# Other steps for the transform pieces of batches one to four and other banks for all of them, in a fused Fourier filter and PReLU feed-forward kernel

## Chip, cores and metric

One core of a Trainium2 chip runs the whole program in one launch. The metric is device time of that launch in microseconds (us). Engines are named PE (matrix multiply; PEld is its weight load), DVE (vector), ACT (scalar), POOL (GpSimd) and SP (sync, which here only issues DMAs). ACT, DVE and POOL run their own queues in order; SP and POOL issue the DMAs of their queues in order too.

## What is computed

```
X = rfft(x, axis=1)                      # x: 8 batches x 3008 positions x 256
y = irfft(X * (filt_r + 1j * filt_i), n=3008, axis=1)
h = y.reshape(24064, 256) @ w_in         # 256 -> 2048
g = maximum(h, 0) + alpha * minimum(h, 0)
out = g @ w_out                          # 2048 -> 256
```

Inputs and outputs are fp32; inside, operands are fp16 and sums fp32.

## The kernel before

**Feed-forward.** 24064 tokens are worked in 48 blocks of 512 tokens (every twelfth, the sixth of each pair of batches, has 384). A block takes 16 steps; step 16n+j computes the j-th group of 128 hidden units of block n (`Block.up`, L478: two 512-wide matmuls into `hps`, two steps share one PSUM tile of the pool psH, which has two). After each odd step ACT copies the pair to `gtb` as fp16 (L486), and DVE applies the PReLU (L489 twice, L490). The second product, by `wout_s`, is a list of single matmuls (`eight`, L515; in the 19 blocks named in FAST `seven`, L537, a variant with 7 products in place of 8, which needs sums from DVE, L498 and L500, and two accumulate DMAs on POOL for each half, L502 and L504). It runs 16 steps (LAG) behind: with each step one sixteenth of a block's list is issued. So block 0 has no such work beside it. Output tiles `osb` (ring of three) are stored by SP (L447).

**Fourier part.** Length 3008 is split as 47 x 64. A batch passes through pieces, each small enough to be put between two steps of the feed-forward:
- `load_x` (L148): POOL issues two DMAs for one of four chunks `xs`; the ring has four, so a chunk of the next batch waits for the same chunk of the batch before.
- `piece_a` (16 of them): one 512-wide matmul (L190) to a psF bank, evicted by ACT to `asb` (L260). After each fourth, `save_a` (SP) writes the chunk to `a_dram`; `asb` has two buffers. `turn_a` (SP) reads all back with positions on partitions, as `at`, in one part or in quarters.
- `piece_b` (12): two 256-wide matmuls (L210), then DVE multiplies the bank twice by the filter (`ww` L213, `uu` L214), and POOL adds `ww` with halves exchanged onto `uu` by two accumulate DMAs (L216). `uu` has four buffers. `ww` uses `filts_s` and `uu` uses `filt_s`, whose upper half must hold the negated lower one: `neg` (DVE, L626) in four parts makes this for batches from 1 on.
- `piece_c` (12): two matmuls by `twi_s` (L228) to a bank, evicted by ACT to `v`. After each third, `turn_c` (SP, four DMAs) writes `v_dram`; after the last of a batch, three loads of `zt` follow (`load_z`, ring of three), the fourth later.
- `piece_d` (16): four 94-wide matmuls (L253) to a bank, evicted by ACT to `yT` (128 features x tokens), which the feed-forward reads. Four of these serve 752 tokens.

Batch 0 has its own path (`First`), run ahead of the steps up to its first quarter of `yT`; of its remaining pieces, `piece_t` (transposes, L331) and `piece_d` 4 to 15, some are evicted by DVE in place of ACT. `combine` (DVE, five instructions) prepares sums of `wout_s` for the FAST blocks, whose first is block 12, at step 192.

**Order.** Everything is issued in program order by hand (`manual_schedule`). `plan` maps a step to a list of pieces; `put` appends to it. At a step, first come delayed stores, then the sums of FAST blocks, then the pieces of that step in the order in which they were put, then `up`, then the second product's share. Batches 4 to 7 repeat the lists STEPS_A, STEPS_B, STEPS_C, STEPS_D, shifted by 96 steps each; batches 1 and 2 go through `plan_fft` with regular spacings; batch 3 uses the lists with changed A and B. A batch b is needed from step 96b on.

**Banks.** The pieces of the transform share two PSUM banks, pools psF0 and psF1 with one buffer each. The string BANKS holds one digit for each piece in program order: which of the two it takes. A piece waits until the earlier one on its bank is evicted.

Of the kernel before, what the change touches and what calls it, by code (L numbers as in the profile page):

```python
# [16 lines left out]
NK1 = 24  # L17
D = 256
NB = 8
DFF = 2048  # L20
NH = 32
BANKS = (
    "010101010101010101010101010101001011011011011011011011011010101011010101010101010101010010101010"
    "101010101010101010101101101101010101001011010010110101010101101010101010101001101010101010101010"
    "101001010110101010101010101010101010100110100101010010110111010110101010101010101010101010101001"
    "010101010100101101101010010101010101010101010101010101100101101010110100100010100101010101010101"
    "01010101010101101010101101001110101010101010101010101010"
)
STEPS_A = (-84, -81, -77, -76, -65, -59, -58, -58, -56, -53, -52, -51, -50, -48, -46, -43)
STEPS_B = (-21, -15, 4, 6, 13, 21, 25, 27, 32, 40, 54, 55)  # L30
STEPS_C = (2, 10, 16, 19, 24, 33, 35, 46, 62, 63, 70, 70)
STEPS_D = (89, 89, 90, 91, 92, 94, 95, 98, 100, 101, 105, 113, 118, 125, 144, 147)
FAST = frozenset([n for n in range(12,42) if n%6 in (0,2,4)]+[42,43,44,45])
SUMS = ((9, 1, 0), (10, 3, 0), (16, 2, 0), (17, 1, 1), (17, 3, 1), (19, 2, 1), (20, 4, 0), (21, 4, 1))
TAIL = ((12, 1, 0), (12, 3, 0), (18, 1, 1), (18, 3, 1), (18, 2, 0), (18, 2, 1), (20, 4, 0), (21, 4, 1))
LAG = 16
# [44 lines left out]
def kernel(  # L81
# [10 lines left out]
    nc = tc.nc  # L92
# [48 lines left out]
    def xrow(b, h, c):  # L141
        return bass.AP(tensor=x.tensor, offset=x.offset + (b * NFFT + NH * h + 8 * c) * D,
                       ap=[[N2 * D, N1], [1, 8 * D]])

    def load_x(b, c):
        xs = p_x.tile([2 * N1, 8 * D], FP16, name="xs")
        for h in range(2):
            nc.gpsimd.dma_start(out=xs[h * N1 : h * N1 + N1], in_=xrow(b, h, c))  # L148
        return xs
# [115 lines left out]
    both = (on_act, on_dve)  # L265
# [71 lines left out]
    xc = {(0, c): load_x(0, c) for c in range(4)}  # L337
    f0 = First()
# [116 lines left out]
    def flush():  # L455
        for fn, args in late:
            fn(*args)
        late.clear()

    class Block:  # L460
        def __init__(self, n, p, t0, tn):
            self.n, self.p, self.t0, self.tn = n, p, t0, tn
            self.fast = n in FAST
            self.sent = 0
# [130 lines left out]
    def put(step, fn, *args):  # L595
        plan.setdefault(step, []).append((fn, args))

    def plan_fft(b, a0, ga, ta, b0, gap, add, lag, d0, quarters, x_at):
        f = Fft(b)
        for i in range(16):  # L600
            put(int(a0 + ga * i) - (b == 2 and i == 7), f.piece_a, i, on_act)
        for c in range(4):
            put(int(a0 + ga * (4 * c + 3)) - (b == 2 and c == 1), f.save_a, c)
            if b + 1 < NB:
                put(x_at[c],
                    lambda b=b, c=c: xc.update({(b + 1, c): load_x(b + 1, c)}))
        for q in range(quarters):
            w = NK1 // quarters
            put(ta, f.turn_a, nc.sync, w * q, w * q + w)
        bs = [b0 + (2 * int(gap * kp / 2) if add else int(gap * kp)) for kp in range(12)]  # L610
        for kp in range(12):
            put(bs[kp], f.piece_b, kp)
            put(bs[kp] + lag, f.piece_c, kp, on_act)
        for q in range(4):
            put(bs[3 * q + 2] + lag + 1, f.turn_c, q)
        for i in range(16):
            put(d0 + min(i, 4) + 2 * max(i - 4, 0), f.piece_d, i, on_act)
        put(d0 + 5, f.load_z, 3)

    for g, t0, d0, gap, evs in ((1, 0, 6, 1, both), (2, 17, 25, 2, (on_dve,)), (3, 32, 40, 2, (on_act,))):  # L620
        for i in range(4):
            put(t0 + gap * i, f0.piece_t, 4 * g + i, evs[i % len(evs)])
            put(d0 + gap * i, f0.piece_d, 4 * g + i, evs[i % len(evs)])

    def neg(ka, kb):
        nc.vector.tensor_scalar(filt_s[64:128, ka:kb], filt_s[0:64, ka:kb], -1.0, None, OP.mult)  # L626

    for i in range(4):
        put(26 + 3 * i, neg, 6 * i, 6 * i + 6)
    plan_fft(1, 16, 1, 32, 40, 3, 0, 6, 92, 4, (20, 24, 74, 75))  # L630
    plan_fft(2, 66, 2, 97, 109, 4.5, 8, 12, 187, 4, (110, 114, 118, 122))
    for b in range(3, NB):
        p = 96 * (b - 1)
        f = Fft(b)
        steps_a = STEPS_A if b > 3 else [int(2.4 * i) - 68 for i in range(16)]
        steps_b = STEPS_B if b > 3 else [max(st, 2 * kp - 12) for kp, st in enumerate(STEPS_B)]
        for i in range(16):
            put(p + steps_a[i], f.piece_a, i, on_act)
            if i % 4 == 3:
                put(p + steps_a[i] + 1, f.save_a, i // 4)  # L640
        if b + 1 < NB:
            for c in range(4):
                put(p - 8 + 4 * c, lambda b=b, c=c: xc.update({(b + 1, c): load_x(b + 1, c)}))
        put(p + steps_a[15] + 4, f.turn_a, nc.sync)
        for kp in range(12):
            put(p + steps_b[kp], f.piece_b, kp)
            put(p + STEPS_C[kp], f.piece_c, kp, on_act)
            if kp % 3 == 2:
                put(p + STEPS_C[kp] + 1, f.turn_c, kp // 3)
        for i in range(16):  # L650
            put(p + STEPS_D[i], f.piece_d, i, on_act)
        put(p + STEPS_D[3] + 2, f.load_z, 3)

    def combine(n):
        b11, b12, b21, b22 = (wout_s.rearrange("p (k e) (h c) -> p e h k c", e=2, h=2)[:, e, h]
# [11 lines left out]
            nc.vector.tensor_sub(t3, b22, b12)  # L667

    for n in range(5):
        put(130 + 3 * n, combine, n)  # L670
    blk, todo, ahead = Block(-2, 0, 0, 0), [], {}
    done = 0.0
    for n, (p, t0, tn, _) in enumerate(blocks):
        old, blk = blk, Block(n, p, t0, tn)
        if blk.fast:
            for at, w, h in SUMS if n < 39 else TAIL:
                ahead.setdefault(16 * n + at, []).append((blk, w, h))
        for j in range(16):
            step = 16 * n + j
            flush()  # L680
            for b, w, h in ahead.pop(step, ()):
                assert w > 2 or not old.fast or b is old or old.sent >= 88 - 16 * w + 8 * h
                b.sums(w, h)
            for fn, args in plan.pop(step, ()):
                fn(*args)
            blk.up(j)
            while todo and done < (step - LAG) / 16:
                try:
                    done += next(todo[0])
                except StopIteration:  # L690
                    todo.pop(0)
        todo.append(blk.items())
# [36 lines left out]
```

## Time and profile before

| what | value |
|---|---|
| median of three runs | 787.47 us (786.89 to 788.47) |
| profiled execution, whole | 784.66 us |
| its span | 782.9 us |
| granted PE clock | 1.00 |
| HBM traffic | 56.06 MB read, 46.66 MB written |
| step 0 / 16 / 32 / 96 / 192 begin | 36.8 / 47.6 / 68.2 / 138.8 / 234.4 us |

The span runs from the first instruction to the last; 1.8 us of the profiled execution lie around it. Some 37 us pass before step 0 (constants, the start of batch 0), 746 us hold the 768 steps and the tail. In a line of busy times by stretch, the fields are the window, its length, the busy time (and instruction count) of PE, PEld, DVE, ACT and POOL, the granted clock, the mean share of 16 DMA engines and GB/s. In a line of waits: who waited for whom, the sum in us, how often, the longest. In a group line: line, engine, operation, tiles, count, then busy us, mean ns of one, and the idle time just before them.

| group | count | mean ns of one |
|---|---|---|
| L486 ACT, copy of an hps pair | 384 | 1007 |
| L260 ACT, eviction of piece_a / piece_c / piece_d | 112 / 84 / 120 | 593 / 598 / 494 |
| L213, L214 DVE, the two products of piece_b | 84 each | 684, 682 |
| L489, L490 DVE | 768, 384 | 349, 681 |
| L626 DVE, neg | 4 | 554 |
| L216 POOL, issue of a uu DMA | 168 | 1010, and 3.1 us from issue to landing |
| L148 POOL, issue of an x load | 64 | 1048, and 8.1 us from issue to landing |

### The profile page before, as it was taken

To read this page: it belongs to the slowest core of one execution; us is meant where nothing else is said; L and a number is where in the kernel's file an instruction comes from. 1 tells how busy PE (TensorE), PEld (TensorE's weight loads), DVE (VectorE), ACT (ScalarE), POOL (GpSimd) and SP (SyncE) were. 2 spreads that over 40 slices of the span, in tenths; PEclk is the share of its full clock that TensorE was granted. 3 is DMA by queue.
4 is the path that set the end of the run, shared out by engine and by line. 5 is a ranking of instruction groups with operands and counts; after the bars stand their busy time and mean duration, and the time that the engine had idled before them with its cause. 6 is when DMAs were issued, how large, how long until landed. Compare 5 with 4: busy or idle time off the path is not lost.

```text
span 782.9 us, 18110 instructions
## 1 busy us (share of the span) xinstructions
PE 760.3 (97%) x6856; PEld 539.0 (69%) x6856; DVE 681.2 (87%) x1489; ACT 603.8 (77%) x896; POOL 266.0 (34%) x353
## 2 busy tenths in 40 slices
PE   7899999999999999999999999999999999999998
PEld 6757657666667666766767767767677777767766
DVE  4798986789788989899899989989899999879994
ACT  4788678878778887788868887778878777687763
POOL 7720542153232522543325423534222433102210
PEclk9999999999999999999999999999999999999999
DMA  9995558685596779985899769886797555635642
GB/s 188 194 214 160 110 111 202 185 159 119 130 209 131 138 165 197 215 171 113 180 225 178 145 137 199 196 164 129 167 199 175 115 108 91 172 89 109 123 97 67
DMA packets 113807, 120.84 MB, mean 154 GB/s; under 512 B 12648, under 2 KB 94328, under 8 KB 113592
## 3 DMA queue, kind: packets, MB, share of 16 engines
q0 software_dynamic: 33584, 50.09, 39.4%
q1 hardware_dynamic: 79992, 69.52, 33.2%
q8 instruction: 54, 0.88, 0.5%
q14 instruction: 33, 0.27, 0.1%
q10 hardware_dynamic: 144, 0.07, 0.0%
HBM read 56.06 MB, written 46.66 MB: 131 GB/s over the span
## 4 chain that ended last, share of the span: by engine, by line
PE 78%; DVE 8%; DMA 8%; ACT 3%; issue 2%; POOL 1%; SPq 1%; DVEq 0%; ACTq 0%; POOLq 0%
PE hps L478 34%; PE op L515 20%; PE op L537 12%; PE psF L190 3%; DMA uu<-ww 3%; DVE m L489 2%; PE psF L253 2%; PE psF L228 2%; DVE gtb L490 2%; PE psF L210 2%; DMA out_dram<-osb 2%; ACT gtb L486 2%; DMA twf_s<-c_twf 1%; DMA gtb<-ss 1%; DVE ww L213 1%
## 5 line engine op out<-in xcount | busy, mean ns | idle before, releaser
L486 ACT ACTIVATE gtb<-hps 128x1024 f16<-128x1024 f32 (+1 forms) x384 | 386.5, 1007 | 107.4 <-PE hps L478 104.9
L478 PE MATMUL hps<-yT,win_s 128*128 128x512 f16 (+1 forms) x1536 | 449.2, 374 | 0.4 <-ACT gtb L486 0.2
L489 DVE TENSOR_SCALAR m<-gtb,alm_s 128x512 f16<-128x512 f16 (+1 forms) x768 | 235.3, 349 | 60.2 <-ACT gtb L486 57.9
L490 DVE TENSOR_TENSOR gtb<-gtb,m 128x1024 f16<-128x1024 f16 (+1 forms) x384 | 261.6, 681 | 17.9
L515 PE MATMUL op<-wout_s,gtb 128*128 128x256 f16 x1728 | 262.0, 272 | 0.0
L515 PEld LDWEIGHTS <-gtb 128*128 128x128 f16 x1728 | 168.4, 97 | 113.5
L216 POOL DMA_DIRECT2D uu<-ww x168 | 140.7, 1010 | 278.4 <-DVE uu L214 102.7
L478 PEld LDWEIGHTS <-win_s 128*128 128x128 f16 x1536 | 137.3, 98 | 27.1 <-issue 3.6
L537 PEld LDWEIGHTS <-gtb 128*128 128x128 f16 x1520 | 103.4, 98 | 48.7 <-DMA gtb<-ss 1.3
L502 POOL DMA_DIRECT2D gtb<-gtb x38 | 37.5, 987 | 175.5 <-DVE ss L498 71.7
L537 PE MATMUL op<-wout_s,gtb 128*128 128x128 f16 x912 | 76.9, 219 | 1.6 <-DMA gtb<-ss 1.1
L260 ACT ACTIVATE asb<-psF 96x512 f16<-96x512 f32 x112 | 65.9, 593 | 13.5 <-PE psF L190 13.0
L260 ACT ACTIVATE yT<-psF 128x376 f16<-128x376 f32 x120 | 58.7, 494 | 7.7 <-PE psF L253 7.2
L260 ACT ACTIVATE v<-psF 128x512 f16<-128x512 f32 x84 | 49.7, 598 | 13.1 <-PE psF L228 12.6
L213 DVE TENSOR_TENSOR ww<-psF,filts_s 128x512 f16<-128x512 f32 x84 | 57.4, 684 | 0.0
L214 DVE TENSOR_TENSOR uu<-psF,filt_s 128x512 f16<-128x512 f32 x84 | 57.3, 682 | 0.0
L537 PEld LDWEIGHTS <-ss 128*128 128x128 f16 x608 | 42.6, 98 | 20.9
L537 PE MATMUL op<-tw_s,gtb 128*128 128x128 f16 x608 | 52.5, 219 | 0.0
L537 PE MATMUL op<-tw_s,ss 128*128 128x128 f16 x608 | 52.5, 219 | 0.0
L148 POOL DMA_DIRECT2D xs<-in_x_dram x64 | 41.7, 1048 | 22.4 <-PE psF L190 13.2
L190 PE MATMUL psF<-xs,wf_s 94*96 94x512 f16 x112 | 42.0, 381 | 2.4 <-ACT v L260 0.9
L253 PE MATMUL psF<-wi_s,zt 96*128 96x94 f16 x504 | 41.1, 204 | 3.2 <-ACT yT L260 2.8
(85 smaller groups left out, 507.4 us busy)
## 6 DMA issues: line engine op xcount, KB each, us to landing
out_dram<-osb SPq DMA_DIRECT2D x127, 128.0 KB
xs<-in_x_dram POOLq DMA_DIRECT2D x64, 188.0 KB, 8.1
a_dram<-asb SPq DMA_DIRECT2D x28, 384.0 KB
uu<-ww POOLq DMA_DIRECT2D x168, 64.0 KB, 3.1
v_dram<-v SPq DMA_DIRECT2D x112, 96.0 KB
zt<-v_dram SPq DMA_DIRECT2D x28, 384.0 KB
gtb<-gtb POOLq DMA_DIRECT2D x38, 256.0 KB, 3.9
gtb<-ss POOLq DMA_DIRECT2D x38, 256.0 KB, 6.2
```

Of the source, the lines that this page charges most:

```text
L190: nc.tensor.matmul(ps[0:96], wf1_s, xs[:, o : o + 512], start=True, stop=True)
L213: nc.vector.tensor_mul(ww, px, filts_s[:, 2 * kp : 2 * kp + 2])
L214: nc.vector.tensor_mul(uu, px, filt_s[:, 2 * kp : 2 * kp + 2])
L216: nc.gpsimd.dma_start(out=uu[o : o + 64], in_=ww[64 - o : 128 - o], accum_op=OP.add)
L253: nc.tensor.matmul(ps[:, m], self.zt[g][:, 4 * mh + m, dh * 128 : dh * 128 + 128], wi3_s, start=True, stop=True)
L260: nc.scalar.activation(o, i, AF.Copy)
L478: nc.tensor.matmul(self.hps[:, j % 2, 0:tn], win_s[:, kt, j * 128 : (j + 1) * 128], yT[:, kt, self.t0 : self.t0 + tn], start=(kt == 0), st ...
L486: nc.scalar.activation(g, hs, AF.Copy)
L489: nc.vector.tensor_scalar(ms[:, i], g[:, i], 0.0, a, OP.min, OP.mult)
L490: nc.vector.tensor_add(g, g, ms)
L515: nc.tensor.matmul(op[:, si % 2], self.pair(k // 2)[:, k % 2, 128 * si : 128 * si + 128], wout_s[:, k], start=(k == 0), stop=(k == 15))
L537: nc.tensor.matmul(acc[:, 128 * i : 128 * i + 128], x[:, k, 128 * i : 128 * i + 128], b[:, k], start=first and k + i == 0, stop=k == 7, sk ...
```

## The change

Steps of batches 1, 2 and 3 come from written lists (FIRST), as do those of batch 0's remaining pieces (STEPS_T, STEPS_E), the sign copies (STEPS_N), the weight sums (STEPS_K) and the x loads of batches 2 and 3 (STEPS_X, in steps from the start). `plan_fft` goes. FAST is written out, and the condition for TAIL gets a second half. BANKS has new digits (left out below; the first 24, of the part ahead of the steps, are the same).

```diff
-FAST = frozenset([n for n in range(12,42) if n%6 in (0,2,4)]+[42,43,44,45])
+STEPS_T = (0, 1, 3, 3, 19, 21, 21, 23, 32, 32, 34, 36)
+STEPS_E = (7, 7, 10, 12, 25, 25, 27, 29, 40, 41, 44, 50)
+STEPS_N = (33, 35, 35, 57)
+STEPS_K = (134, 137, 141, 167, 198)
+STEPS_X = ((27, 48, 52, 59), (97, 115, 116, 142))
+FIRST = (
+    ((9, 10, 11, 13, 15, 16, 16, 18, 19, 20, 20, 22, 24, 28, 30, 31),
+     (41, 41, 44, 45, 49, 53, 55, 55, 61, 64, 69, 72),
+     (48, 49, 52, 53, 59, 61, 67, 68, 70, 73, 76, 80),
+     (93, 94, 94, 95, 98, 101, 102, 105, 107, 107, 109, 118, 119, 120, 121, 128)),
+    ((-31, -28, -27, -24, -21, -19, -18, -17, -12, -10, -10, -8, -8, -6, -5, 0),
+     (13, 17, 17, 27, 31, 33, 33, 41, 46, 51, 52, 61),
+     (21, 28, 31, 37, 39, 43, 43, 51, 54, 61, 66, 76),
+     (91, 91, 93, 93, 95, 97, 99, 100, 102, 104, 106, 107, 113, 124, 126, 130)),
+    ((-70, -66, -66, -60, -59, -58, -56, -55, -52, -51, -50, -48, -40, -38, -38, -34),
+     (-12, -10, 0, 13, 15, 20, 25, 29, 33, 40, 46, 54),
+     (-1, 7, 12, 24, 26, 29, 33, 50, 63, 64, 64, 69),
+     (90, 90, 92, 93, 93, 95, 95, 95, 100, 110, 118, 119, 125, 126, 148, 152)),
+)
+FAST = frozenset((12, 14, 16, 18, 20, 22, 24, 26, 28, 30, 32, 34, 36, 38, 40, 42, 43, 44, 45))
...
-    def plan_fft(b, a0, ga, ta, b0, gap, add, lag, d0, quarters, x_at):
...
-    for g, t0, d0, gap, evs in ((1, 0, 6, 1, both), (2, 17, 25, 2, (on_dve,)), (3, 32, 40, 2, (on_act,))):
-        for i in range(4):
-            put(t0 + gap * i, f0.piece_t, 4 * g + i, evs[i % len(evs)])
-            put(d0 + gap * i, f0.piece_d, 4 * g + i, evs[i % len(evs)])
+    for i in range(12):
+        ev = both[i % 2] if i < 4 else (on_dve, on_act)[i // 8]
+        put(STEPS_T[i], f0.piece_t, 4 + i, ev)
+        put(STEPS_E[i], f0.piece_d, 4 + i, ev)
...
-        put(26 + 3 * i, neg, 6 * i, 6 * i + 6)
-    plan_fft(1, 16, 1, 32, 40, 3, 0, 6, 92, 4, (20, 24, 74, 75))
-    plan_fft(2, 66, 2, 97, 109, 4.5, 8, 12, 187, 4, (110, 114, 118, 122))
-    for b in range(3, NB):
+        put(STEPS_N[i], neg, 6 * i, 6 * i + 6)
+    for b in range(1, NB):
         p = 96 * (b - 1)
         f = Fft(b)
-        steps_a = STEPS_A if b > 3 else [int(2.4 * i) - 68 for i in range(16)]
-        steps_b = STEPS_B if b > 3 else [max(st, 2 * kp - 12) for kp, st in enumerate(STEPS_B)]
+        steps_a, steps_b, steps_c, steps_d = FIRST[b - 1] if b < 4 else (STEPS_A, STEPS_B, STEPS_C, STEPS_D)
...
-                put(p + steps_a[i] + 1, f.save_a, i // 4)
+                put(p + steps_a[i] + (b > 2), f.save_a, i // 4)
...
-                put(p - 8 + 4 * c, lambda b=b, c=c: xc.update({(b + 1, c): load_x(b + 1, c)}))
-        put(p + steps_a[15] + 4, f.turn_a, nc.sync)
+                put(STEPS_X[b - 1][c] if b < 3 else p - 8 + 4 * c,
+                    lambda b=b, c=c: xc.update({(b + 1, c): load_x(b + 1, c)}))
+        quarters, later = (4, 1) if b < 3 else (1, 4)
+        w = NK1 // quarters
+        for q in range(quarters):
+            put(p + steps_a[15] + later, f.turn_a, nc.sync, w * q, w * q + w)
...
-        put(130 + 3 * n, combine, n)
+        put(STEPS_K[n], combine, n)
...
-            for at, w, h in SUMS if n < 39 else TAIL:
+            for at, w, h in SUMS if n < 39 and n - 1 not in FAST else TAIL:
```

The arguments of `plan_fft` were: batch, step and spacing of piece_a, step of turn_a, first step and spacing of piece_b, a number that rounds them to even distances, steps from piece_b to piece_c, first step of piece_d, parts of turn_a, steps of the four x loads. So batch 1 had piece_a at steps 16 to 31, piece_b at 40, 43, ..., 73, piece_c six steps after each, piece_d from 92 on; batch 2 piece_a at 66 to 96, piece_b at 109 to 157, piece_c twelve steps after, piece_d from 187 on.

More of the change, by code (lines that the diff above doesn't have):

```diff
@@ L22 @@
 BANKS = (
[L23 to L27, printed above, removed]
+    "010101010101010101010101010101001010010101101010101010101010101010101011010101010001011011101010"
+    "101010101010101010101010101010010101010101010010101101011010101010101010100101010101011010010010"
+    "110100101001010010101010101010101010101010001010110101101001010110101010101001010101010101010110"
+    "101010101011010010010101101010101010101010101010101010011010010101001011011101011010101010101010"
+    "10101010101010010101010010110001010101010101010101010101"
 )
@@ L596, in put @@
         plan.setdefault(step, []).append((fn, args))
-    def plan_fft(b, a0, ga, ta, b0, gap, add, lag, d0, quarters, x_at):
[L599 to L618, printed above, removed]
-    for g, t0, d0, gap, evs in ((1, 0, 6, 1, both), (2, 17, 25, 2, (on_dve,)), (3, 32, 40, 2, (on_act,))):
-        for i in range(4):
-            put(t0 + gap * i, f0.piece_t, 4 * g + i, evs[i % len(evs)])
-            put(d0 + gap * i, f0.piece_d, 4 * g + i, evs[i % len(evs)])
+    for i in range(12):
+        ev = both[i % 2] if i < 4 else (on_dve, on_act)[i // 8]
+        put(STEPS_T[i], f0.piece_t, 4 + i, ev)
+        put(STEPS_E[i], f0.piece_d, 4 + i, ev)
     def neg(ka, kb):
@@ L639 @@
             if i % 4 == 3:
-                put(p + steps_a[i] + 1, f.save_a, i // 4)
+                put(p + steps_a[i] + (b > 2), f.save_a, i // 4)
         if b + 1 < NB:
             for c in range(4):
-                put(p - 8 + 4 * c, lambda b=b, c=c: xc.update({(b + 1, c): load_x(b + 1, c)}))
-        put(p + steps_a[15] + 4, f.turn_a, nc.sync)
+                put(STEPS_X[b - 1][c] if b < 3 else p - 8 + 4 * c,
[4 more added lines that the diff above has]
+            put(p + steps_a[15] + later, f.turn_a, nc.sync, w * q, w * q + w)
         for kp in range(12):
             put(p + steps_b[kp], f.piece_b, kp)
-            put(p + STEPS_C[kp], f.piece_c, kp, on_act)
+            put(p + steps_c[kp], f.piece_c, kp, on_act)
             if kp % 3 == 2:
-                put(p + STEPS_C[kp] + 1, f.turn_c, kp // 3)
+                put(p + steps_c[kp] + 1, f.turn_c, kp // 3)
         for i in range(16):
-            put(p + STEPS_D[i], f.piece_d, i, on_act)
-        put(p + STEPS_D[3] + 2, f.load_z, 3)
+            put(p + steps_d[i], f.piece_d, i, on_act)
+        put(p + steps_d[3] + 2, f.load_z, 3)
     def combine(n):
```

## The prediction

> **What bounds the kernel now.** I read the engine totals first, then the chain that ended last, then busy time by stretches cut at block starts, then what TensorE (PE) waits for in each stretch, and last the timeline around the longest waits.
>
> ```profile
> PE 760.3 (97%) x6856; PEld 539.0 (69%) x6856; DVE 681.2 (87%) x1489; ACT 603.8 (77%) x896; POOL 266.0 (34%) x353
> ...
> PE 78%; DVE 8%; DMA 8%; ACT 3%; issue 2%; POOL 1%; SPq 1%; DVEq 0%; ACTq 0%; POOLq 0%
> ```
>
> PE is the bound, and the chain runs over it for 78% of the span. What a re-placing of steps can win is the rest: places where PE waits. The stretches say where these are (PE busy is the first number after the length):
>
> ```profile
> 36.00:47.60 11.60, 10.51 (x72) 5.78 (x73) 9.71 (x23) 9.38 (x14) 2.62 (x5) 1.00 1.17 220
> 47.60:68.20 20.60, 19.77 (x144) 13.31 (x143) 17.73 (x39) 16.71 (x26) 2.04 (x4) 1.00 0.77 181
> 68.20:86.00 17.80, 16.64 (x133) 11.69 (x133) 15.01 (x32) 12.80 (x20) 3.37 (x4) 1.00 0.60 156
> 86.00:104.50 18.50, 17.25 (x124) 11.54 (x122) 16.58 (x36) 12.90 (x17) 9.50 (x12) 1.00 0.54 106
> 104.50:123.70 19.20, 17.84 (x122) 11.68 (x120) 14.81 (x31) 15.19 (x23) 9.42 (x13) 1.00 0.63 119
> ...
> 328.00:783.00 455.00, 448.75 (x4215) 319.26 (x4213) 413.39 (x916) 352.97 (x519) 142.86 (x172) 1.00 0.70 146
> ```
>
> The granted clock is 1.00 throughout, so clock is no part of this. From 36 to 124 us (steps 0 to 79) PE is idle 1.1, 0.8, 1.2, 1.3 and 1.4 us; from 328 us on nearly never, until the tail. What is waited for, in steps 32 to 96 and then in 139 to 328 us:
>
> ```profile
> PE psF L228 <- DMA uu<-ww: 3.2, 5, 1.1
> PE psF L190 <- ACT v L260: 0.5, 1, 0.5
> ...
> PE psF L253 <- ACT yT L260: 0.8, 1, 0.8
> PE psF L190 <- DVE uu L214: 0.7, 1, 0.7
> ```
>
> One of them close up, on the timeline (start, length, engine):
>
> ```profile
> 82.22 1.65 POOL L216 DMA_DIRECT2D uu<-ww  x2 [0.72 <-DVE uu L214]
> 82.54 0.33 PE L253 MATMUL psF<-wi_s,zt 96*128 96x94 f16 x4
> 83.93 0.39 PE L228 MATMUL psF<-uu,twi_s 128*128 128x256 f16 x2 [1.06 <-DMA uu<-ww]
> ```
>
> piece_c of batch 1 stands six steps behind its piece_b, and the accumulate DMA between them lands late. A listed end is modelled: L515 x4 takes 0.60 us on the timeline while one is listed with 272 ns, so starts are (0.60-0.27)/3 = 0.109 us apart. I therefore count a wait from start to start over the usual pitch (0.216 us for a 512-wide, 0.109 for a 256-wide matmul, 0.042 for one of L253); above, 1.2 us instead of the listed 1.06. Counted so, with all above 0.08 us, PE loses 3.6 us in steps 0-31, 5.3 in 32-95 (2.9 before five piece_c, the rest at banks and zt), 1.9 in 96-191, 2.2 in 192-287, 0.3 in 288-330: 13.2 us. That is the most that the change can give there; after step 330 the three long waits (1.3 at 510 us on gtb<-ss, 1.4 at 684, 0.4 at 747) belong to batches whose steps do not move.
>
> **What is not changed in effect.** FAST lists the same 19 blocks. The new test for TAIL asks whether the block before is in FAST: below block 39 all FAST blocks are even and their predecessors odd, so SUMS stays for them. Every instruction stays, in number and shape; turn_a's quarters for batch 3 stay one, for 1 and 2 four. Batches 4 to 7 keep their steps and mostly get the other bank of the two throughout, which exchanges two equal buffers: 0.
>
> **The prices.** ACT evictions 0.59 (asb, v, zt) and 0.49 us (yT), the ACT copy of an hps pair 1.02; DVE 1.29 for ww and uu (0.68+0.61 between starts), 1.23 per pair of steps for m and gtb (0.54+0.69), 0.68 for a combine, 0.55 for a neg. PE pieces: a, b, c 0.22, d 0.17, t 0.30; a step without pieces 0.43 (L478) + 0.44 (L515). A psF bank is taken again after that eviction. At an even step the hps copy of the odd step before is still 0.8 us long on ACT, so a piece there is free 1.4 us (d: 1.3) after its matmul starts; with one piece and one step between, PE comes back after 1.3. The row: at step 66-67, exactly so, it lost 0.12; with a bank taken twice in one step (70, 156, 211) 0.63, 0.63, 0.51. These two calibrate what follows.
>
> **Steps 0-31** (now 3.6). Five piece_a move from steps 16-31 into block 0, where no L515 work runs yet. PE work there rises from 8.8 to 9.9, ACT from 10.3 to 13.3 us (five times 0.59), DVE stays at 12.0; steps 16-31 fall to PE 17.7, ACT 15.9, DVE 14.1. Block 0 becomes ACT's (about 12.2 us instead of 10.8 from step 0 to 16, counting from the first copy at 38.27), block 1 PE's: 17.7 + 0.6 for three short banks (steps 16, 20, 21) against the measured 20.6. Together 30.7 against 31.4: gain 0.7; ends 0 (ACT's queue serial) and 2 (PE's 27.6 + 1.8 for the start). The cover is DVE's backlog of 2 us at step 16, which now meets piece_t 9 and 10 at step 21; no more than its wait now (0.5 at step 18).
>
> **Steps 32-95** (now 5.3). The lag from b to c goes from 6 steps to 7-13. The chain it must hold, from rows: PE 0.2, DVE 0 to 0.7 of waiting and 1.29, POOL 0.3+0.55, landing 2.3 to 3.7: 5.0 to 6.8 us. Six steps are 5.2 + 0.5 for pieces; seven are 6.1 + 1.0, eight 6.9 + 1.3. So the 2.9 of the five waits go. But x loads of batch 2 now stand on POOL's queue before uu 4, 5 and 8 (steps 48, 52, 59; two DMAs of 0.5 to 1.05 us each), and beside x loads at 153-166 us uu landed after 3.7 to 5.0; uu 5 has eight steps (8.0 us) for up to 8.5: 0 to 1 lost, I take 0.3, c5 being the only one without room. New bank waits, at steps: 41 (piece_b 1 on the bank of piece_d 13 in the same step) 0.5; 49 and 53, 0.1 each; 55 (two piece_b; DVE has 20.2 us of work in steps 40-55 for PE's 17.1, so b7 waits for b5's two products) 0.5; 69, 0.1 + 0.4 (piece_a 2 right behind piece_a 1's bank); 73, 0.15; 95, 0.1; zt stays 0.3 (turn_c to piece_d 12 steps in both). Sum 2.5, gain 2.8; ends 1 and 4.5.
>
> **Steps 96-191** (now 1.9: DVE at 128 and 132 where five combines fall beside piece_b, banks at 150, 156). Two combines leave for 167 and 198, where DVE has 10.5 and 16.9 us in 16 steps against PE's 14.3 and 16.6. No bank is taken twice in a step. But steps 128-143 hold 17.5 PE, 17.0 ACT, 17.0 us DVE (now 16.9, 15.9, 17.1): I take 1.3 lost (128-129 0.4, 133-139 0.6, 117-121 0.3), gain 0.6; ends -1 and 1.5. The loads of batch 3, chunk 3 (step 142 for use at 152) wait only for POOL's uu 7 of step 137, and land 5 to 6 us after issue. On SP, save_a, turn_a and turn_c move by 0 to 3 steps; zt of batch 2 was issued at 222.8 us, step 179, for step 187, so three steps later still leaves some 3 us.
>
> **Steps 192-330** (now 2.5). The 1.0 at step 281 (ACT held by L551 until 322 us for an osb store, two piece_d behind it) goes, since piece_d moves one step behind the copy; the double bank at 211 goes (0.5), and 0.6 at 198, 212 and 261. New: step 287, three piece_d of which the third takes the first's bank at once, 0.5; 222-223, 0.4; 205-207, 0.4; 302-303 and 310-311, 0.3 each behind even piece_d. And on POOL uu 5 of batch 3 (step 212) comes between the two L504 of block 12: the second went at 257.5 and landed at 266.4, used near step 224 (268.1 us); it now goes some 2.5 us later: 0 to 1, I take 0.3. Sum 2.2 + 0.4 for what remains at 292 and 304: gain about 0; ends -1.5 and 1.
>
> The sum: 0.7 + 2.8 + 0.6 + 0 = 4.1, rounded to 3.9 for small bank waits under 0.08. **784.7 - 3.9 = 780.8 us** by the profiled execution's own time (span 782.9). The median of the runs shown is 787.5, 2.8 above it; carried over, 783.6.
>
> The page "Perfetto Trace Analysis" of the Trainium skill, "Identifying the Most-Contended Engine", says the engine of highest occupancy is the one to optimize, and that for TensorE weight loads tell more than matmul time. By it DVE (87%) would bound, not PE (69% of weight loads), and a change that leaves DVE's work alone would give nothing. The trace differs: in 123.7-138.8 us DVE was busy 8.98 of 15.10 while PE never paused for more than 0.3. I give it weight within the first rival.
>
> **Rivals.**
> - *The waits only move* (0.15). Piece_c no longer waits, but bank and queue waits take its place: 3.6 again in steps 0-31 (ACT's order), 4.3 in 32-95 (all upper ends), 2.9 in 96-191, 2.6 after: 13.4, that is 784.9, or 787.7 as a median. For it: DVE's 20.2 against 17.1 in steps 40-55, and the three engines level in 128-143. Against: each wait found so far is a place one can name, and fewer are left.
> - *Stores hold ACT* (0.14; slower). SP serves saves, turns and stores in order; where a moved turn_c or save_a waits for ACT, the stores of osb behind it leave late, and the next osb copy (L551) holds ACT, as at 684.8 us (1.74 idle, PE 1.4 late). If all five FAST blocks 12 to 20 met this, 780.8 + 5 x 1.4 = 787.8, median 790.6. From three such waits on (4.2) nothing is gained, from four it is slower. Against it: now only three of 19 blocks show it (3.4 us in all), and batch 3's turns move by at most four steps.
> - *Nearly all waits go* (0.10): half of my 9.3 remaining too: 776.2, median 779.0. For it: lags of 8 and more everywhere. Against: step 287 and 41 are certain.
> - Forecast, 0.61, its own range 1.6 to 6.3 gained: median 781.2 to 785.9.
>
> About 0.2% (1.6 us) can be told from no change. Faster: 0.61 + 0.10, less 0.01 for the forecast's weak end: 0.70; same 0.16; slower 0.14. The range 779.4 to 788.4 leaves out most of the slower case and half of the best one: some 0.2.
>
> **What will show it.** Right: PE's wait for DMA uu<-ww between steps 32 and 96 falls from 3.2 to under 1; step 32 is reached near 67.5 instead of 68.2 us, step 96 near 135.3 instead of 138.8, step 192 near 230.3 instead of 234.4; PE waits for ACT yT near step 287. From step 330 on the same length as now. Wrong: a uu wait at piece_c 5 over 1 us, ACT osb L551 waiting for stores in more than three blocks, or step 96 later than 137.5.

## The result, and the profile after

| | before | after |
|---|---|---|
| median | 787.31 us (4 runs) | 793.21 us (4 runs, 791.7 to 795.53) |
| ratio | | 1.0066, 95% interval 1.0042 to 1.009 |
| profiled execution, its span | 784.66, 782.9 us | 793.42, 791.6 us |
| steps 0-31 | 31.4 us | 41.1 us |
| steps 32-95 | 70.6 us | 67.9 us |
| steps 96-191 | 95.6 us | 95.1 us |
| steps 192-335 | 140.8 us | 141.3 us |
| step 336 to the end | 407.7 us | 409.0 us |

The change made the kernel slower by 0.66%. The stages, cut where the first L478 (after: L497) of a step starts, sum with the start (step 0 at 36.8 and 37.2 us) to the whole difference of the spans, 8.7 us: +9.7 in the first 32 steps, -3.2 in the next 160, +1.8 after. So the first 32 steps hold more than the whole loss, the next 160 gain, and 1.8 us of loss lie behind step 192.

Totals and chain of the page, after:

```profile
PE 762.3 (96%) x6856; PEld 541.3 (68%) x6856; DVE 682.4 (86%) x1489; ACT 604.1 (76%) x896; POOL 265.6 (34%) x353
...
PE 75%; DMA 10%; DVE 5%; ACT 4%; POOL 3%; issue 2%; SPq 1%; DVEq 0%; ACTq 0%; POOLq 0%
```

Every engine has as many instructions as before; in the chain, DMA rises from 8% to 10% of the span and PE falls from 78% to 75%. Stretches after, cut at the same blocks as before (window, length, PE, PEld, DVE, ACT, POOL, clock, DMA share, GB/s):

```profile
37.20:50.50 13.30, 11.11 (x69) 5.69 (x68) 10.44 (x25) 11.65 (x17) 3.63 (x7) 1.00 1.14 222
50.50:78.30 27.80, 20.29 (x143) 13.52 (x142) 15.39 (x34) 14.30 (x21) 0.00 (x0) 0.88 0.41 101
78.30:95.30 17.00, 16.33 (x129) 11.56 (x129) 15.24 (x32) 11.89 (x18) 4.12 (x6) 1.00 0.63 162
95.30:113.30 18.00, 16.86 (x125) 11.51 (x123) 17.62 (x39) 12.67 (x18) 13.03 (x19) 1.00 0.91 157
113.30:131.00 17.70, 17.60 (x122) 11.77 (x120) 14.55 (x31) 15.36 (x24) 7.65 (x10) 1.00 0.69 148
```

Block 1 (second line) takes 27.8 us where it took 20.6, with PE idle for 7.5 of them and a clock of 0.88. Blocks 2 to 4 (the other three) are shorter than before, 52.7 against 55.5 us. What PE waits for in steps 0 to 31, and then in 32 to 96, after:

```profile
PE psF L209 <- ACT asb L279: 7.5, 1, 7.5
PE psF L209 <- DMA xs<-in_x_dram: 0.8, 1, 0.8
...
PE psF L247 <- DMA uu<-ww: 1.1, 2, 0.9
PE psF L229 <- ACT yT L279: 0.7, 1, 0.7
PE psF L272 <- DMA zt<-v_dram: 0.4, 1, 0.4
```

One wait of 7.5 us. ACT, which PE waits for, was not busy; the timeline shows it idle too, and the chain shows what for:

```profile
61.44 0.59 ACT L279 ACTIVATE asb<-psF 96x512 f16<-96x512 f32 x1 [8.12 <-DMA a_dram<-asb]
62.09 1.01 PE L209 MATMUL psF<-xs,wf_s 94*96 94x512 f16 x2 [7.47 <-ACT asb L279]
```

```profile
48.04 0.60 ACT asb L279
48.64 0.02 issue
48.66 12.70 DMA a_dram<-asb
61.36 0.02 issue
```

piece_a 8 (step 19) opens the third chunk. `asb` has two buffers, so its eviction overwrites chunk 0, whose `save_a` (step 13) must have been read out. That save is issued at 48.66 us and lands only at 61.36. ACT runs in order: the hps copies queue behind the eviction, PE comes to piece_a 9, which takes the bank that piece_a 8 still holds, and both stop. Before, the same save was issued at 53.0 and landed at 58.6 us by the semaphore's updates in the trace, and chunk 2 began at step 24. This is its first eviction, before:

```profile
58.79 0.59 ACT L260 ACTIVATE asb<-psF 96x512 f16<-96x512 f32 x1
```

The room was 0.2 us.

And the wait costs more than its length. The clock in windows around it, after:

```profile
54.00:62.00 8.00, 0.62 (x5) 0.41 (x4) 0.80 (x2) 0.56 (x2) 0.00 (x0) 0.84 0.67 174
62.00:66.00 4.00, 3.91 (x18) 2.39 (x18) 2.04 (x5) 1.92 (x4) 0.00 (x0) 0.50 0.00 0
66.00:70.00 4.00, 4.00 (x29) 2.64 (x28) 2.60 (x6) 2.70 (x4) 0.00 (x0) 0.96 0.28 79
```

After 7.5 us without work PE runs at a granted clock of 0.50 for about 4 us: 512-wide matmuls start 0.43 us apart in place of 0.216. The late starts in those 4 us sum to 2.0 us. The page "TensorE: Matmul & The Clock Gate" of the Trainium skill, "Part 1: The HAM clock gate", has the clock at half after an idle window of about 3.4 us, until about as long a busy one; the trace agrees, with 0.50 at 62 to 66 us and 0.96 in the next four. So this one wait cost 7.6 (start to start) + 2.0 us, about the whole 9.7. Of the smaller waits, which replace the 3.6 us that the prediction counted there before, the longest, 1.0, is piece_a 0, which at step 9 waited for its x load (landed at 43.7 us).

What POOL had issued before the save (timeline after):

```profile
43.65 0.53 POOL L439 DMA_DIRECT2D twi_s<-tw_s  x1 [0.99 <-PE hps L497]
44.17 0.54 POOL L441 DMA_DIRECT2D filts_s<-filt_s  x1
44.99 0.52 POOL L441 DMA_DIRECT2D filts_s<-filt_s  x1 [0.29 <-DMA xs<-in_x_dram]
48.15 1.04 POOL L167 DMA_DIRECT2D xs<-in_x_dram  x2 [2.64 <-PE psF L209]
```

The copies of the filter, 768 KB each, land at 55.0 and 58.6 us; the x load, which the early piece_a 3 has set free, at 60.2 and 61.6. Before, the copies landed at 52.8 and 56.0 us and the save behind them at 58.6; so the save, issued some 4 us earlier than before, lands 2.8 us later. Which of these transfers makes the save late is the first question of the experiments.

### The profile page after: what moved, and what is told of

Its sections match the earlier page's. It is cut to its first block, busy times and chain, and to the rows that moved or that the text cites. A ratio compares the mean times of both kernels' runs of the same rounds, so it can differ in the third digit from the quotient of the medians.

```text
span 791.6 us, 18095 instructions
## 1 busy us (share of the span) xinstructions
PE 762.3 (96%) x6856; PEld 541.3 (68%) x6856; DVE 682.4 (86%) x1489; ACT 604.1 (76%) x896; POOL 265.6 (34%) x353
## 4 chain that ended last, share of the span: by engine, by line
PE 75%; DMA 10%; DVE 5%; ACT 4%; POOL 3%; issue 2%; SPq 1%; DVEq 0%; ACTq 0%; POOLq 0%
PE hps L497 34%; PE op L534 21%; PE op L556 11%; PE psF L209 3%; DMA xs<-in_x_dram 2%; PE psF L272 2%; PE psF L247 2%; ACT gtb L505 2%; PE psF L229 2%; DMA uu<-ww 2%; DMA a_dram<-asb 2%; DVE m L508 2%; DVE gtb L509 1%; DMA out_dram<-osb 1%; DMA gtb<-ss 1%
## 5 line engine op out<-in xcount | busy, mean ns | idle before, releaser
L497 PE MATMUL hps<-yT,win_s 128*128 128x512 f16 (+1 forms) x1536 | 450.3, 375 | 0.3 <-ACT gtb L505 0.2
L497 PEld LDWEIGHTS <-win_s 128*128 128x128 f16 x1536 | 137.4, 98 | 26.1 <-issue 2.8
L279 ACT ACTIVATE v<-psF 128x512 f16<-128x512 f32 x84 | 49.5, 598 | 12.5 <-PE psF L247 11.9
L167 POOL DMA_DIRECT2D xs<-in_x_dram x64 | 44.0, 1120 | 13.7 <-PE psF L350 4.5
```

Source lines behind the costliest of these rows:

```text
L279: nc.scalar.activation(o, i, AF.Copy)
L497: nc.tensor.matmul(self.hps[:, j % 2, 0:tn], win_s[:, kt, j * 128 : (j + 1) * 128], yT[:, kt, self.t0 : self.t0 + tn], start=(kt == 0), st ...
```

## Experiments

All are the changed kernel with one thing different, unless said otherwise. Steps are given in us at which they begin.

| run | time | against before | step 0 | 16 | 32 | 96 | 192 | 336 | span |
|---|---|---|---|---|---|---|---|---|---|
| before | | | 36.8 | 47.6 | 68.2 | 138.8 | 234.4 | 375.2 | 782.9 |
| after | 793.21 | 1.0066 | 37.2 | 50.5 | 78.3 | 146.2 | 241.3 | 382.6 | 791.6 |
| e1_own_buffers | 784.86 | 0.9973 (0.9953 to 0.9992) | 37.0 | 49.5 | 68.1 | 136.2 | 230.8 | 372.3 | 781.7 |
| e2_x_later | 792.85, one run | | 37.4 | 49.9 | 76.0 | 145.1 | 239.9 | 381.5 | 791.1 |
| e3_chunks_back | 790.22, one run | | 37.4 | 49.9 | 71.3 | 137.4 | 233.2 | 374.8 | 788.4 |
| e4_copies_behind | 792.46, one run | | 36.5 | 49.0 | 76.1 | 144.1 | 239.7 | 381.0 | 790.7 |
| e5_copies_after_x | 787.07, one run | | 37.3 | 50.1 | 71.2 | 138.5 | 233.5 | 375.6 | 785.2 |
| e6_more_places | 782.57 | 0.9956 (0.994 to 0.9972) | 37.6 | 50.1 | 68.7 | 137.2 | 231.7 | 372.2 | 780.1 |
| e7_x_loads | 784.46, one run | | 36.6 | 50.1 | 68.7 | 136.5 | 231.1 | 372.9 | 782.7 |
| e8_x_between | 781.40 | 0.9928 (0.9901 to 0.9955) | 37.0 | 49.6 | 68.1 | 135.0 | 229.9 | 370.0 | 781.1 |

**e1_own_buffers: take the ring away.**

```diff
-                self.asb[i // 4] = p_as.tile([96, 8, D], FP16, name="asb")
+                if self.b == 1 and i > 7:
+                    self.asb[i // 4] = ss[0:96, i // 4 - 2]
+                else:
+                    self.asb[i // 4] = p_as.tile([96, 8, D], FP16, name="asb")
```

> The changed kernel, but chunks 2 and 3 of batch 1's piece_a are evicted into two halves of ss (idle until block 12), so that ACT needs no asb buffer back from save_a. Theory A (the ring of two asb buffers: ACT waits 8.1 us for the save of chunk 0, PE loses 7.6 us behind it and about 1.4 us more at half clock): both go, step 32 falls from 78.3 to 68-69.5 us, the median from 793.2 to 783.5-785.5, that is 0.995 to 0.998 of the kernel before. Rival B (block 0 is held by DVE and ACT work as such, and the wait for the save only stands where another would): step 32 stays above 72 us and the median above 787.

Block 1 and steps 32 to 95 in e1_own_buffers, and the two longest waits of PE in it from 36 to 78 us:

```profile
49.50:68.10 18.60, 18.55 (x143) 12.82 (x142) 15.35 (x34) 14.36 (x21) 0.00 (x0) 1.00 0.62 160
68.10:136.20 68.10, 65.56 (x490) 45.70 (x489) 56.47 (x124) 52.73 (x80) 24.82 (x32) 1.00 0.73 162
```

```profile
PE psF L212 <- DVE yT L285: 0.7, 2, 0.5
PE psF L232 <- ACT yT L282: 0.7, 1, 0.7
```

Block 1 takes 18.6 us with 18.55 of PE work, at full clock, although the save lands just as late (issued 47.7, landed 59.8 us). Step 32 comes at 68.1, and the ratio to the kernel before is 0.9973 in place of 1.0066: with an interval of 0.9953 to 0.9992 the kernel is now a little faster than the one before. Theory A holds, rival B falls: the wait for the ring was more than the whole net loss.

**e2_x_later, e3_chunks_back: what makes the save late, and when it is needed.**

```diff
-STEPS_X = ((27, 48, 52, 59), (97, 115, 116, 142))
+STEPS_X = ((46, 48, 52, 59), (97, 115, 116, 142))
```

> The changed kernel with the load of chunk 0 of batch 2 named at step 46 instead of 27, so that POOL issues it behind the first uu transfers and no x load stands near the save at 48.7 us. Theory A1 (the save is late because the two filts_s copies and what else POOL issued before it fill the DMA engines): it still lands at 58-61 us, ACT waits at least 5 us, and step 32 at 75-78 us. Rival A2 (the x load of batch 2, issued at 48.2 us just ahead of the save, is what delays it): the wait falls below 3 us, step 32 to 69-72 us.

```diff
-    ((9, 10, 11, 13, 15, 16, 16, 18, 19, 20, 20, 22, 24, 28, 30, 31),
+    ((9, 10, 11, 13, 15, 16, 16, 18, 24, 25, 26, 27, 28, 29, 30, 31),
```

> The changed kernel with piece_a 8 to 15 of batch 1 back at steps 24 to 31; pieces 0 to 7 stay early. Theory A: the third chunk is now needed some 5 steps later, about 57.5 us, while the save of chunk 0 lands at 58 to 61.4, so the wait shrinks to 1-4 us: step 32 at 70-74 us. Rival B: no less than 76 us, since the early pieces 0 to 4 in block 0 cost as before.

ACT's wait in e2_x_later:

```profile
ACT asb L279 <- DMA a_dram<-asb: 6.2, 1, 6.2
```

Without the x load the save takes 10.8 us from issue (48.1) to landing (58.9) instead of 12.7, and the wait is 6.2 instead of 8.1: the x load is some 2 us of it, the rest is not, as A1 expected. Step 32 at 76.0 fits, and A2 falls. In e3_chunks_back step 32 comes at 71.3, inside the theory's 70 to 74, but not for its reason: no wait of 1 to 4 us for the save is left. Banks that now meet other pieces cost 1.7 and 1.1 us at steps 21 and 25, and behind the first of these waits chunk 2 is evicted only from 60.3 us on, 0.1 us after the save landed. Its whole time says little, since a wait of 3.1 us for gtb<-ss at step 480, where no piece of the edit stands, is in it (0.6 in the changed kernel).

**e4_copies_behind, e5_copies_after_x: order on POOL's queue.** Both move the two filts_s copies into the plan:

```diff
-    for o in (0, 64):
-        nc.gpsimd.dma_start(out=filts_s[o : o + 64], in_=filt_s[64:128])
...
+    def copies():
+        for o in (0, 64):
+            nc.gpsimd.dma_start(out=filts_s[o : o + 64], in_=filt_s[64:128])
+
+    put(14, copies)
...
-STEPS_X = ((27, 48, 52, 59), (97, 115, 116, 142))
+STEPS_X = ((14, 48, 52, 59), (97, 115, 116, 142))
```

> The changed kernel with the two filts_s copies issued by POOL behind the load of chunk 0 of batch 2 (both named at step 14), so about 49 us instead of 44.2 us and after the save of chunk 0. Theory A1 (what POOL issued before the save is served first): the save then lands 4-6 us after its issue, near 54 us, ACT's wait falls below 2 us, step 32 at 69-71.5 us. Rival A2 (only the x load matters) or A3 (all transfers share alike whatever their order): the save lands at 58 us or later, and the wait stays above 4 us.

It was inconclusive: within step 14 the copies were put before the x load, and a step's name holds back nothing on POOL, which goes on as soon as its own waits allow. They were issued at 42.1 and 43.2 us, ahead of the save as in the changed kernel (the save, issued at 47.2, landed at 58.7 us; step 32 came at 76.1). With `put(14, copies)` moved below the batches' loop they stand behind the load, which does wait:

> The changed kernel with the two filts_s copies standing on POOL's queue right behind the load of chunk 0 of batch 2, which waits for piece_a 3, so that they are issued about 48 to 49 us instead of 43 to 44, about when the save of chunk 0 is. In the run before this one the copies were meant to stand there but were put ahead of the load, so POOL issued them at 42.1 and 43.2 us as ever, and nothing was tested. Theory A1 (the save waits for what POOL issued before it): it lands within 7 us of its issue, by 55.5 us, ACT's wait falls below 2.5 us, step 32 at 69-72 us. Rival A3 (everything under way shares the DMA engines, so the order of issue does not matter): the save lands at 58 us or later, the wait stays above 4.5 us and step 32 above 74 us.

POOL's timeline, and ACT's wait, in e5_copies_after_x:

```profile
47.81 1.04 POOL L167 DMA_DIRECT2D xs<-in_x_dram  x2 [4.19 <-PE psF L209]
48.84 1.04 POOL L652 DMA_DIRECT2D filts_s<-filt_s  x2
```

```profile
ACT asb L279 <- DMA a_dram<-asb: 2.4, 1, 2.4
```

The save of chunk 0, issued at 48.3, lands at 52.7 us: 4.4 us in place of 12.7. A1 holds, A3 falls. The 2.4 us are the next save, of chunk 1, which is issued at 53.0 behind the copies, lands at 62.5 and is needed at step 24. The late landing goes with standing behind the copies in the order of issue, not with the save. What of the copies holds a save up, that they were issued first or that their packets are long, these runs do not separate: the first save of e5 moved beside packets of the x load.

**e6_more_places, e7_x_loads, e8_x_between: do the other waits come away too?** These start from e1_own_buffers. e6:

```diff
-STEPS_E = (7, 7, 10, 12, 25, 25, 27, 29, 40, 41, 44, 50)
+STEPS_E = (7, 7, 10, 12, 25, 25, 27, 29, 38, 39, 44, 50)
-STEPS_X = ((27, 48, 52, 59), (97, 115, 116, 142))
+STEPS_X = ((27, 34, 74, 75), (97, 115, 116, 142))
-     (-1, 7, 12, 24, 26, 29, 33, 50, 63, 64, 64, 69),
-     (90, 90, 92, 93, 93, 95, 95, 95, 100, 110, 118, 119, 125, 126, 148, 152)),
+     (-1, 7, 12, 24, 26, 31, 33, 50, 63, 64, 64, 69),
+     (90, 90, 92, 93, 93, 95, 95, 97, 100, 110, 118, 119, 125, 126, 148, 154)),
```

Steps are counted here by the lists; for waits the expectations name the step before, in which PE waits (52 for a piece of step 53). Digits of BANKS follow their pieces to the new order; one piece, piece_a 4 of batch 4, takes the other bank.

> The kernel of e1_own_buffers with five more places moved: x loads of batch 2 at steps 27, 34, 74, 75 (none between the uu transfers of batch 1); piece_d 12 and 13 of batch 0 at 38 and 39 (not in the step of two piece_b); in batch 3 piece_c 5 two steps later, piece_d 7 two and piece_d 15 two. By the waits of e1_own_buffers: uu at steps 52 and 60 (0.6 + 1.1), the bank at 40 (0.8), uu at 220 (1.3), banks at 286 (0.6) and 343 (1.5), in all 5.9 us; some 0.5 to 1 comes back at the new places. Theory (each wait is its own and PE bounds all else): median 4 to 5.5 us below e1_own_buffers, 779.5-781, ratio to the kernel before 0.990 to 0.9935. Rival (DVE and ACT, level with PE in steps 40 to 143, hold it anyway): less than 2 us is won and the ratio stays above 0.995.

e7 has the line of STEPS_X alone, e8 is e6 with `(27, 34, 59, 65)` there.

> The kernel of e1_own_buffers with the x loads of batch 2 at steps 27, 34, 74, 75 alone. Theory X (the waits for uu at steps 52 and 60, 0.57 and 1.10 us, come from x loads on POOL's queue and on the DMA engines ahead of the uu transfers): both fall below 0.3, steps 32 to 96 take 66.4-67 us instead of 68.1. Rival (the lag of eight steps is too short because DVE has 20.2 us of work in steps 40 to 55): at least 1 us of the two stays.

> The kernel of e6_more_places with the last two x loads of batch 2 at steps 59 and 65 instead of 74 and 75, so that they land before the writes to v_dram and the loads of zt of batch 1 (steps 80 to 92). Theory (the wait for zt at step 92 grew from 0.6 to 1.8 us since x loads near 119 us stand in its way): it falls to 0.6 or less, and no uu wait over 0.4 comes at steps 60 to 80; step 96 at 135.5-136.3 us instead of 137.2, counted with step 0 at 37.6, and the median 0.7 to 1.5 below 782.6. Rival (zt is late because piece_c 11 is, twelve steps are too few): the wait stays above 1.2.

In e7 both uu waits are gone, as theory X had it, but steps 32 to 95 take 67.8 us, not 66.4 to 67. PE now waits 1.75 us by starts for zt at step 93 (0.6 in e1). The x loads, now issued at 116 to 119 us, landed up to 127.9, while batch 1's last writes to v_dram were issued at 124.1 to 126.0. e8 tests whether they lie in the way. PE's longest wait from 78 to 147 us in e7, and then the two longest in e8:

```profile
PE psF L275 <- DMA zt<-v_dram: 1.6, 1, 1.6
```

```profile
PE psF L232 <- DVE uu L236: 0.7, 2, 0.4
PE psF L250 <- DMA uu<-ww: 0.2, 1, 0.2
```

In e6 the theory's 4 to 5.5 us did not come: its median is 2.3 us below e1's, by the ratios (0.9956 and 0.9973) it is 1.3 us, and the two intervals overlap. By starts e6 lost 0.6, 0.8 and 1.8 us at steps 44, 53 and 93, while the waits at 287 and 344 went and the one at 221 fell from 1.3 to 0.3 us. So the waits are not as independent as the theory took them. The rival's ratio above 0.995 came out; whether less than 2 us was won is not decided.

With the x loads between the two (e8) PE waits 0.3 us for zt, which shows them as the cause of that wait. Step 96 comes at 135.0 us with step 0 at 37.0, and the median is 781.40, 1.2 below that of e6: within the 0.7 to 1.5 us expected. e8's ratio, 0.9928, has its whole interval below 1. It has the lowest median, but its interval overlaps that of e6, whose profiled span is 1.0 us shorter: from step 336 on e8 takes 411.1 us and e6 407.9, though e8 moved nothing there.

## Why the prediction was wrong

Gains are positive and losses negative here.

- **Steps 0 to 31, forecast 0.7, came out -9.7.** The failed step is the costing of the five early piece_a: "gain 0.7; ends 0 (ACT's queue serial) and 2". It priced what they do on PE and ACT and named DVE's backlog as cover, but a moved piece_a also moves the use of its buffer: chunk 2 went from step 24 to 19, and the save of chunk 0 from step 19 to 13, behind POOL's copies. The sum had no term for `asb`, and the saves were looked at only for steps 96 to 191 ("move by 0 to 3 steps"). No end of that range held a wait for a landing; the runs show one of 7.6 us and 2.0 us of slow clock behind it. With that wait away (e1) the same steps take 31.1 us for 31.4: 0.3 gained, block 0 12.5 us (12.2 forecast) and block 1 18.6 (18.3). These two forecasts add up to 30.5, not to the 30.7 that the prediction has, so even its own terms were 0.6 better than what e1 reached.
- **Steps 32 to 95, forecast 2.8, came out 2.7.** The mechanism was mostly right: uu waits fell from 3.2 to 1.1 us, just above the "under 1" that was to show it. That the sums agree is in part luck. Single terms were off both ways: piece_c 5 lost 1.1 (0.3 taken, 0 to 1 its ends), the bank at step 41 0.8 (0.5), zt 0.6 (0.3); piece_b 7 at step 55 lost nothing (0.5). piece_c 5 was not the only one without room: piece_c 3 waited 0.4 us, also eight steps behind its piece_b. The low end of that chain adds up to 4.6 us by its own terms, not 5.0; no term rests on it. e7 shows the cause of the uu waits, the x loads between them.
- **Steps 96 to 191, forecast 0.6, came out 0.5**, and 1.0 in e1.
- **Steps 192 to 330, forecast 0, came out -0.7.** Step 281's wait went and step 287's came, 0.57 for 0.5. The second L504 was not late; instead piece_c 4 and 5 themselves, eleven and nine steps behind their piece_b, waited 0.55 and 1.1 us for uu at steps 218 and 221.
- **From step 330 on, forecast 0, came out -1.1** (-1.3 from step 336). piece_d 15 of batch 3 at step 344 took the bank of piece_b 10 of batch 4, whose second product DVE began only at 391.1 us: 1.5 us by starts. It is one of the change's own places, and was left out since the stretch of the prediction ended at 330. With that place moved (e6) the wait is gone and the time from step 336 on is 407.9 us, as before. PE's wait there, after:

```profile
PE psF L272 <- DVE uu L233: 1.3, 1, 1.3
```

- **The signs.** Step 96 came at 146.2 us, later than the 137.5 that was to show the prediction wrong, and PE waited 1.1 us by starts for uu at piece_c 5, where more than 1 was to show it.
- **The rivals.** The slower one, stores that hold ACT, is not what happened: ACT's L551 (after: L570) waited for stores 1.7 us in one wait, where it was 3.4 us in three waits before. It was near, though: ACT was held by a ring whose reader had not landed, but the ring was `asb` and not `osb`. So the chance of 0.14 for a slower kernel did not stand on the cause that made it slower. That waits only move was partly seen in e6 and e7. That DVE, as the engine of highest occupancy, bounds is not borne out: e8 wins 0.7% with every DVE instruction kept. The section that the prediction draws on there, "Identifying the Most-Contended Engine" of the page "Perfetto Trace Analysis" of the Trainium skill, names the share of peak FLOPs beside the weight loads for TensorE; the prediction went by the weight loads alone.

## What to carry to other kernels

When a piece is moved ahead, list each ring that it takes a buffer from, and ask for the buffer's last reader what must land by then, and behind which transfers it is issued; the work of the piece alone says nothing of that. A margin of 0.2 us on such a ring is found by comparing a landing with the next use, since no wait in the profile shows it. A stall of several us on PE is to be charged with the slow clock after it, here 2.0 us behind one of 7.5.

## What was not expected of the hardware

**A save hardly moved while the copies did.** These are the DMA queues of the changed kernel from 48.66 to 54 us, and of e5 from 48.3 to 52.7 us (packets, MB, their time as a share of 16 engines); q0 is POOL's queue and q1 holds the save:

```profile
q0 software_dynamic: 117, 1.15, 106.1%
q1 hardware_dynamic: 2, 0.01, 0.6%
...
q0 software_dynamic: 134, 0.47, 67.8%
q1 hardware_dynamic: 112, 0.39, 22.4%
```

In the first, 90 of q0's packets are rows of 12 KB of the copies, 0.9 us each, and the save gets 2 packets in 5.3 us. In the second, 85 are of 4 KB and 2 of 12 KB, and q1 gets 112. e5's second save, issued at 53.0 us behind the copies, has its first packet only at 59.3. The page "DMA: Bandwidth & Descriptors" of the Trainium skill, "Queues, rings and completion order", says that each engine goes round the queues that have work and takes a whole packet, typically 9 to 17 descriptors, from one before it turns to the next. The first trace shows no such turns between its own packets; but whether a packet of the trace is a packet of that page or only a descriptor of one, no run here shows, so the two need not differ. Why the copies keep the engines stays open.

**A stall shorter than the one above was enough for the slow clock.** After 7.5 us of idle PE ran at clock 0.50 for some 4 us, which made 2.0 us of the loss. In e8 PE waited only 2.3 us, near 680 us. These are the 3.41 us that end with the start of the slow clock, and the 3.41 us after:

```profile
679.50:682.91 3.41, 1.11 (x18) 0.86 (x16) 1.39 (x4) 1.47 (x4) 0.14 (x1) 1.00 1.12 257
682.91:686.32 3.41, 3.41 (x30) 2.74 (x28) 1.96 (x6) 2.75 (x6) 0.00 (x0) 0.50 0.87 198
```

PE was busy for 1.11 us of the first stretch and ran at 0.50 in the second. That is less than the idle window of about 3.4 us that the Trainium skill has by the page cited above, so here the measurement decides. A wait of 1.8 us at the same place in e6 was followed by a clock of 1.00. Where the limit lies between them no run shows.
